# The order in which the first loads of v and of a weight stand in one DMA queue

## The chip, the cores and the metric

The kernel runs on one core of a Trainium2 chip. A core has five engines that run side by side, each with its own instruction queue and in its own order: PE (TensorE, matrix multiplies; its weight loads are listed as PEld), DVE (VectorE), ACT (ScalarE), POOL (GpSimd) and SP (SyncE), which here does nothing but issue DMA transfers. Engines wait for each other, and for transfers, by semaphores. The metric is the device time of one execution in microseconds (us); smaller is better. All times below are microseconds.

## The reference

Attention with a decay by distance for 8 batches, 8 heads, 576 positions and 64 values per head, followed by a two-layer network on the 4608 tokens that come out of it:

```python
scores = scale * np.matmul(q, k.transpose(0, 1, 3, 2))
Dmat = np.where(rel >= 0, gamma[:, None, None] ** rel[None, :, :], 0.0)
attn = np.matmul(scores * Dmat, v)            # (8, 8, 576, 64), float32
x = attn.transpose(0, 2, 1, 3).reshape(4608, 512)
h = x @ w_in                                  # w_in 512 x 2048
g = h * np.clip(h + 3.0, 0.0, 6.0) / 6.0
out = g @ w_out                               # w_out 2048 x 512
```

## The kernel before

**Tiles.** The positions of each batch are cut into four chunks of 128 and a tail of 64; two tails make one more chunk. In each chunk the scores are formed on PE (s), multiplied by a mask on DVE (into `at`), and multiplied by v and by a running state on PE (o). Its result in PSUM, `xp`, is brought by ACT into `xt` (L334), the transposed x of the batch. When the four chunks of a batch are there, the up-projection (u, or h for half of the tokens) multiplies `xt` by w_in in 16 blocks of 128 columns (fc 0 to 15); ACT and DVE make g of it (L356, L361). Then comes the down-projection: p0 to p7 for batch 0 (four accumulators in PSUM that are held until the end of p7, then copied out by ACT, L426, and DVE, L424), products P for the others.

**One written order.** There is no scheduler. The string PROGRAM is a list of short words, and `act` (L632) emits the instructions of each word in turn; each engine runs what falls to it in this order. The words that matter here:

- `L0.0` to `L1.1`: q and k of batch 0, two DMAs of 512 KB each, in runs of 1 KB (L199).
- `V0` to `V3`: v of the first four chunks, one DMA of 256 KB each, in runs of 256 bytes (`load_v`, L241), into tiles `st` of which there are six.
- `W0.i`: the i-th of eight pieces of w_in, 512 KB in runs of 2 KB (`wload`, L530). Piece i holds columns 512·(i//2) onwards (fc 4·(i//2) to 4·(i//2)+3) and half of the rows. Pieces 0 to 3 go into tiles `wst` of which there are four, pieces 4 to 7 into `tmat`, which is not yet used for anything else. `W1.i` is the same for w_out, two fc for each piece.
- `w0.ie`: the cast of such a piece to 16 bits on engine e (v DVE, s ACT, g POOL).
- `cN.2e`: the cast and scaling of chunk N's v; `cN.0e` and `cN.1e` those of its q and k. `lN`: the load of q, k and v of chunk N from 4 on (`load`, L146).
- `H19`: 19 matmuls of zeros that occupy PE while nothing has landed.

All of the loads named are issued on SP, so they stand in one queue, and the order of the words is the order of this queue. Nothing that SP issues in the first 20 us waits for another engine.

**The order around the change.** After the loads the words go on like this (left out are those that touch neither v nor w_in):

```
c0.2g c1.2g ... w0.0s K1v w0.1g ... o0 s2 o1 S3
c2.2g o2 h0.0.0.1 w0.3s c3.2g o3 h0.0.2.3 h0.1.0.1.8 w0.2g ...
w0.5g w0.6g ... h0.1.2.3 ... w0.7s ... w0.4g ... u0.4 u0.5
```

So POOL casts v0 and v1, then W0.1, then v2 and v3, then W0.2, W0.5, W0.6 and W0.4. ACT casts W0.0 before it empties `xp` of chunk 0, and W0.3 before it empties `xp` of chunk 3. The half up-projections `h0.0` need chunks 0 and 1 and the pieces 0 and 1; `h0.1` needs chunks 2 and 3 as well; `u0.4` to `u0.7` need the pieces 2 and 3, `u0.8` the pieces 4 and 5.

**Later places that are spoken of.** `c7.1v` is the cast of chunk 7's k on DVE. It is followed on DVE by `t0 t1` (differences of quarters of w_out, L576), the mask of chunk 6, and the two copies of L424; the half up-projections of batch 1 (`h1.0`) then use the PSUM buffers that these copies free. `p4` needs the cast of W1.4 on POOL.

Of the kernel before, what the change touches and what calls it, by code (L numbers as in the profile page):

```python
# [10 lines left out]
FP32 = mybir.dt.float32  # L11
# [21 lines left out]


PROGRAM = """
L0.0 L0.1 C0.0v L1.0 C0.2v L1.1 C0.1v W0.0 W0.1 V0 V1 H19 V2 V3 W0.4 W0.2
W0.3 X0.0s W0.5 C0.3g X0.1s C1.0v X0.2s X0.3s C1.1v X1.0s X1.1s C1.2v X1.2s
C1.3v X1.3s s0.4 c0.2g c1.2g W0.6 S1 K0s w0.0s K1v w0.1g W0.7 o0 s2 o1 S3
c2.2g o2 h0.0.0.1 w0.3s c3.2g o3 h0.0.2.3 h0.1.0.1.8 w0.2g W1.0 W1.6 W1.1
W1.2 W1.3 w0.5g w0.6g l4 h0.1.2.3 l5 w0.7s W1.7 W1.4 w0.4g W1.5 u0.4 u0.5  # L40
# [43 lines left out]
def kernel(  # L84
# [10 lines left out]
    B, H, S, D = q.shape  # L95
    NTOK, DM = out.shape
    DFF = moe_w_in.shape[1]
    P = 128
# [11 lines left out]
    work = ctx.enter_context(tc.tile_pool(name="work", bufs=2))  # L110
# [30 lines left out]
    stage = {}  # L141
# [1 line left out]
    v16s, s16_of, kns = {}, {}, {}  # L143
    cidx = {}

    def load(c):  # L146
        kind, b, t = c
        st = work.tile([P, 3, H, D], FP32, tag="st", bufs=6, name="st")
        stage[c] = st
        for ix, src in enumerate((q, k, v)):  # L150
            if kind == 0:
                nc.sync.dma_start(
                    st[:, ix, :, :],
                    src[b, :, t * P:(t + 1) * P, :].rearrange("h s d -> s h d"))
            else:
                for z in range(2):
                    nc.sync.dma_start(
                        st[z * TAIL:(z + 1) * TAIL, ix, :, :],
                        src[b + z, :, MAIN:S, :].rearrange("h s d -> s h d"))

    def cast(c, ix, eng):
        kind, b, t = c
        st = stage[c]
        ti = t if kind == 0 else 4
        if ix == 2:
            v16s[c] = work.tile([P, H, D], FP16, tag="v16", bufs=5, name="v16")
        elif c not in qk16s:
            qk16s[c] = work.tile([P, 2, H, D], FP16, tag="qk16", bufs=5,
                                 name="qk16")
        dst = v16s[c] if ix == 2 else qk16s[c][:, ix, :, :]  # L170
        tab = (tq if ix == 0 else tkv)[:, ti, :]
        eng.tensor_tensor(out=dst, in0=st[:, ix, :, :],  # L172
                          in1=tab.unsqueeze(2).to_broadcast([P, H, D]),
                          op=ALU.mult)

    def xpose(c):
        qk = qk16s[c]
        qt = work.tile([P, 8, P], FP16, tag="qkT", bufs=4, name="qkT")
        qkTs[c] = qt
        nc.scalar.dma_start_transpose(  # L180
            qt, qk.rearrange("p a h d -> p (a h d)"))
        kns[c] = qk[:, 1, :, :]
# [6 lines left out]
    def load0(ix, hh):  # L189
        if "st" not in qk0:  # L190
            g_new(0)
            g_new(1)
            qk0["st"] = (gs[0].rearrange("p c n -> p (c n)").bitcast(FP32)
                         .rearrange("p (a h r d) -> p a h r d", a=2, h=H, r=4))
            qk0["16"] = (gs[1][:, 0:8, :]
                         .rearrange("p (a r) n -> p a r n", a=2))
        hs = slice(4 * hh, 4 * hh + 4)
        src = (q, k)[ix][0, hs, 0:MAIN, :]
        nc.sync.dma_start(  # L199
            qk0["st"][:, ix, hs, :, :].rearrange("p h r d -> p h (r d)"),  # L200
            src.rearrange("h (p r) d -> p h (r d)", r=4))

    def cast0(ix, p0, eng):
        hs = slice(2 * p0, 2 * p0 + 2)
        tab = (tq if ix == 0 else tkv)[:, 5:9, hs].rearrange("p r h -> p h r")
        out = (qk0["16"][:, ix, :, :].rearrange("p r (h d) -> p h r d", h=H)
               [:, hs, :, :])
        eng.tensor_tensor(out=out, in0=qk0["st"][:, ix, hs, :, :],
                          in1=tab.unsqueeze(3).to_broadcast([P, 2, 4, D]),
                          op=ALU.mult)  # L210
# [7 lines left out]
    def xpose0(ix, p0, eng):  # L218
        tp = psum.tile([P, 4, P], FP16, tag="mm", bufs=4, name="tp")
        for r in range(4):  # L220
            nc.tensor.transpose(tp[:, r, :],
                                qk0["16"][:, ix, r, p0 * P:p0 * P + P], ident)
        copy(eng, wout16[:, 4 * ix + p0, :].rearrange("z (p r) -> z p r", r=4),
             tp.rearrange("z r p -> z p r"))
        if ix == 1 and p0 == 3:
            for t in range(NC4):
                qkTs[(0, 0, t)] = wout16[:, 0:8, t * P:(t + 1) * P]

    def kback(hh, eng):
        tp = psum.tile([P, 2, HP, P], FP16, tag="mm", bufs=4, name="tp")  # L230
        for a in range(2):
            t = 2 * hh + a
            for p in range(HP):
                nc.tensor.transpose(tp[:, a, p, :],
                                    wout16[:, HP + p, t * P:(t + 1) * P], ident)
            kns[(0, 0, t)] = (wout16[:, 8 + t, :]
                              .rearrange("p (h d) -> p h d", h=H))
        dst = wout16[:, 8 + 2 * hh:10 + 2 * hh, :]
        copy(eng, dst.rearrange("p a (b n) -> p a b n", b=HP), tp)

    def load_v(t):  # L241
        st = work.tile([P, 3, H, D], FP32, tag="st", bufs=6, name="st")
        stage[(0, 0, t)] = st
        nc.sync.dma_start(st[:, 2, :, :], v[0, :, t * P:(t + 1) * P, :]  # L244
                          .rearrange("h s d -> s h d"))

    def warm(ps, n, w=P):
        for _ in range(n):
            nc.tensor.matmul(ps, zero16[:, 0:P], zero16[:, 0:w], start=True, stop=True)

    def xpose_pe(c, tag, eng):
        qk = qk16s[c]
        qt = work.tile([P, 8, P], FP16, tag="qkT", bufs=4, name="qkT")
        qkTs[c] = qt
        kns[c] = qk[:, 1, :, :]
        tp = psum.tile([P, 8, P], FP16, tag=tag,
                       bufs=4 if tag == "mm" else 1, name="tp")
        qf = qk.rearrange("p a h d -> p (a h d)")
        for i in range(8):
            nc.tensor.transpose(tp[:, i, :], qf[:, i * P:(i + 1) * P], ident)  # L260
        if eng == "v":
            nc.vector.tensor_copy(qt, tp)
        else:
            nc.scalar.copy(qt, tp)
# [143 lines left out]
    def down_plain_begin(kb):  # L408
        return [psum.tile([P, DM], FP32, tag="mm", bufs=4, name="po")
                for _ in range(BLK // P)]  # L410
# [140 lines left out]
    def wcast(which, i, eng):  # L551
        st = wst.pop((which, i))
        if which == 0:
            f, cc = i // 2, i % 2
            dst = win16[:, 2 * cc:2 * cc + 2, 512 * f:512 * f + 512]
        else:
            dst = wout16[:, 2 * i:2 * i + 2, :]
        if eng == "v":
            nc.vector.tensor_copy(dst, st)
        elif eng == "s":  # L560
            nc.scalar.copy(dst, st)
        else:
            nc.gpsimd.tensor_copy(dst, st)
# [16 lines left out]
    order = []  # L580
# [51 lines left out]
    def act(w):  # L632
        kind, n, e = w[0], [int(x) for x in w[1:].rstrip("svg").split(".")], w[-1]
        if kind == "H":
            xp = psum.tile([P, HP, P], FP32, tag="xp", name="xp")
            warm(xp.rearrange("p a n -> p (a n)"), n[0], BLK)
        elif kind == "L":
            load0(*n)
        elif kind == "C":
            cast0(*n, ENG[e])  # L640
        elif kind == "X":
            xpose0(*n, e)
        elif kind == "K":
            kback(*n, e)
        elif kind == "V":
            load_v(*n)
        elif kind == "l":
            load(order[n[0]])
        elif kind == "c":
            cast(order[n[0]], n[1], ENG[e])  # L650
        elif kind == "x":
            xpose(order[n[0]])
        elif kind == "y":
            xpose_pe(order[n[0]], "xp", e)
        elif kind in "sS":
            ret1(order[n[0]], *n[1:], two=(kind == "S"))
        elif kind == "o":
            ret2(order[n[0]])
        elif kind == "W":
            wload(*n)  # L660
        elif kind == "w":
            wcast(*n, e)
        elif kind == "t":
            tbuild(n[0])
        elif kind == "e":
            enc(*n)
        elif kind == "u":
            up(*n)
        elif kind == "h":
            up_half(n[0], n[1], n[2:4], *n[4:])  # L670
        elif kind == "p":
            if n[0] == 0:
                plain.extend(down_plain_begin(0))
            down_plain_part(0, plain, 2 * n[0], 2 * n[0] + 2)
            if n[0] == HF - 1:
                down_plain_end(0, plain)
        else:
            product(n[0], PROD[n[1]])
# [31 lines left out]
```

## Time and profile before

| what | us |
|---|---|
| median of 7 runs | 308.58 |
| lowest and highest | 307.82 and 309.42 |
| the profiled execution, its own time | 309.42 |
| span of its profile | 307.3 |
| DVE, ACT, POOL busy | 240.5, 145.6, 105.2 |
| bytes moved, mean rate | 53.93 MB, 176 GB/s |

The span goes from the first to the last instruction of the profile; 2.1 us of the execution lie outside it. A busy time is the sum over an engine's instructions. On PE it is not the time at its peak, since matmuls overlap. In the lines of slices, the span is cut in 40 equal parts of 7.7 us, and each digit is a busy share in tenths (9 is 90% or more); PEclk is the share of its clock that PE was granted. In the chain of work, each line has a start, a length, and an engine with a line of the code ("SPq L244" is SP's instruction that issues a load of v); "DMA x<-y" is the time from an issue to the landing. In the waits, a line says who waited for whom, the total, how many times, and the longest. In a timeline, a line has start, length, engine, line, operation, output and input, shape and count, and in brackets the idle time before it and what ended it. In a table by windows the columns are the stretch, its length, the busy time (and instructions) of PE, PEld, DVE, ACT and POOL, PE's granted clock, the busy share of the DMA engines, and GB/s.

### The profile page before, as it was taken

How to read it: one execution, taken by the hardware profiler on the slowest of the kernel's cores; microseconds unless marked ns; L12 is line 12 of the kernel's file. 1: busy time of each engine (PE TensorE's matmuls, PEld its weight loads, DVE VectorE, ACT ScalarE, POOL GpSimd, SP SyncE). 2: the span in 40 equal slices, each digit the busy share in tenths (PEclk: the TensorE clock that was granted, in tenths of full speed). 3: DMA queues.
4: the chain of work that ended last, by engine and by line, in shares of the span. 5: the costliest groups of instructions: out<-in, count | busy, mean ns of one | idle time of the engine just before them, and what ended most of it. 6: DMA issues, size and time to landing. Idle time of an engine off the chain costs nothing.

```text
span 307.3 us, 7129 instructions
## 1 busy us (share of the span) xinstructions
PE 291.9 (95%) x2879; PEld 200.6 (65%) x2879; DVE 240.5 (78%) x341; ACT 145.6 (47%) x267; POOL 105.2 (34%) x116
## 2 busy tenths in 40 slices
PE   8788999897999799999999999999999999999995
PEld 3565444686888688746864686468755874684484
DVE  6655844989985898788878997898699768866963
ACT  2576714764135753377237522763276326405710
POOL 5055536767056745536654141333300000000000
PEclk9779999999999999999999999999999999999999
DMA  7999999999999999999999998995602030014003
GB/s 236 278 272 383 270 280 212 228 205 212 201 174 217 216 208 236 191 207 211 237 211 243 249 230 197 246 221 71 188 2 55 18 127 9 1 36 102 2 0 137
DMA packets 149728, 53.93 MB, mean 176 GB/s; under 512 B 134848, under 2 KB 145088, under 8 KB 149696
## 3 DMA queue, kind: packets, MB, share of 16 engines
q1 hardware_dynamic: 120128, 46.15, 68.7%
q10 hardware_dynamic: 29568, 7.34, 17.8%
q8 instruction: 22, 0.36, 0.5%
q14 instruction: 10, 0.08, 0.1%
HBM read 36.70 MB, written 9.44 MB: 150 GB/s over the span
## 4 chain that ended last, share of the span: by engine, by line
PE 84%; SPq 5%; DVE 4%; DMA 3%; ACT 1%; POOL 1%; issue 0%; ACTq 0%; POOLq 0%
PE ph L373 31%; PE accB L487 9%; PE accA L487 9%; PE accC L487 9%; PE ph L389 7%; PE accD L487 5%; PE po L416 4%; PE xp L304 4%; SPq L244 3%; PE sc L279 3%; DMA wst<-in_moe_w_in_dram 3%; DVE g L361 2%; PE xp L310 1%; POOL qk L172 1%; DVE ss L451 1%; PE state L329 1%
## 5 line engine op out<-in xcount | busy, mean ns | idle before, releaser
L356 ACT ACTIVATE u<-ph 128x512 f32<-128x512 f32 x144 | 84.7, 597 | 66.9 <-PE ph L373 37.1
L361 DVE SCALAR_TENSOR_TENSOR g<-u,ph 128x512 f16<-128x512 f32 x144 | 94.8, 683 | 27.4 <-ACT u L356 26.3
L373 PE MATMUL ph<-xt,win 128*128 128x512 f16 x368 | 82.1, 379 | 0.0
L373 PEld LDWEIGHTS <-win 128*128 128x128 f16 x432 | 41.4, 98 | 47.8
L487 PEld LDWEIGHTS <-ss 128*128 128x128 f16 x512 | 49.1, 98 | 6.8 <-DVE ss L451 0.8
L172 POOL TENSOR_TENSOR v<-st,tkv 128x512 f16<-128x512 f32 x29 | 33.6, 1163 | 39.8 <-DMA st<-in_v_dram 15.8
L172 POOL TENSOR_TENSOR qk<-st,tq 128x512 f16<-128x512 f32 x29 | 31.1, 1071 | 46.8 <-PE state L329 18.3
L290 DVE TENSOR_TENSOR at<-sc,mask 128x1024 f16<-128x1024 f32 (+1 forms) x34 | 39.0, 1155 | 5.7 <-PE sc L279 5.6
L487 PEld LDWEIGHTS <-g 128*128 128x128 f16 x384 | 36.9, 98 | 6.9 <-issue 1.7
L389 PE MATMUL ph<-xt,win 128*128 128x256 f16 x288 | 33.5, 274 | 2.7 <-ACT xt L334 2.7
L172 POOL TENSOR_TENSOR qk<-st,tkv 128x512 f16<-128x512 f32 x26 | 29.6, 1139 | 10.5 <-DMA st<-in_k_dram 10.3
L487 PE MATMUL accA<-wout,g 128*128 128x256 f16 x256 | 30.6, 273 | 1.7 <-DVE g L361 1.7
L389 PEld LDWEIGHTS <-win 128*128 128x128 f16 x288 | 27.7, 98 | 6.8 <-issue 3.0
L487 PE MATMUL accB<-tmat,ss 128*128 128x256 f16 x256 | 30.7, 273 | 0.1
L334 ACT ACTIVATE xt<-xp 128x512 f16<-128x512 f32 x32 | 19.1, 597 | 20.0 <-PE xp L310 17.2
L451 DVE TENSOR_TENSOR ss<-g 128x1024 f16<-128x1024 f16 (+1 forms) x30 | 23.5, 794 | 0.3
L304 PE MATMUL xp<-at,v 128*64 128x128 f16 x288 | 20.6, 228 | 1.5 <-ACT xt L334 0.8
L304 PEld LDWEIGHTS <-v 128*64 128x64 f16 x288 | 14.5, 111 | 7.3 <-issue 4.3
L507 ACT COPY osb<-accA 128x512 f32<-128x512 f32 x8 | 4.7, 586 | 28.2 <-PE accA L487 28.2
L340 ACT CAST s<-state 64x256 f16<-64x256 f32 x48 | 17.3, 361 | 0.5
L416 PE MATMUL po<-wout,g 128*128 128x512 f16 x64 | 15.0, 379 | 0.6 <-DVE g L361 0.5
L487 PE MATMUL accD<-tmat,g 128*128 128x256 f16 x128 | 15.3, 273 | 0.0
(88 smaller groups left out, 274.3 us busy)
## 6 DMA issues: line engine op xcount, KB each, us to landing
st<-in_v_dram SPq DMA_DIRECT2D x32, 256.0 KB, 6.2
out_dram<-osb SPq DMA_DIRECT2D x32, 256.0 KB, 4.5
st<-in_q_dram SPq DMA_DIRECT2D x28, 256.0 KB, 5.5
st<-in_k_dram SPq DMA_DIRECT2D x28, 256.0 KB, 5.9
wst<-in_moe_w_in_dram SPq DMA_DIRECT2D x4, 512.0 KB, 8.9
tmat<-in_moe_w_in_dram SPq DMA_DIRECT2D x4, 512.0 KB, 10.0
wst<-in_moe_w_out_dram SPq DMA_DIRECT2D x4, 512.0 KB, 10.4
g<-in_moe_w_out_dram SPq DMA_DIRECT2D x4, 512.0 KB, 6.6
```

The lines of the kernel that those rows point to most:

```text
L172: eng.tensor_tensor(out=dst, in0=st[:, ix, :, :], in1=tab.unsqueeze(2).to_broadcast([P, H, D]), op=ALU.mult)
L290: nc.vector.tensor_tensor(out=dst, in0=src, op=ALU.mult, in1=m[:, :].unsqueeze(1).to_broadcast([P, n, P]))
L304: nc.tensor.matmul(xp[rows[z], p, :], vt[:, 2 * p + z, :], at[:, z, p, :], start=(p == 0), stop=False, skip_group_check=True)
L334: nc.scalar.activation(xts[b][:, :, t * P:(t + 1) * P], xp, ACTF.Copy, scale=0.125)
L340: nc.scalar.copy(s16[rows[z], :, rows[z]], sp[rows[z], :, :])
L356: nc.scalar.activation(u, ph, ACTF.Relu, bias=0.5, scale=1.0 / 6.0)
L361: nc.vector.scalar_tensor_tensor(out=dst, in0=uv, scalar=1.0, in1=pv, op0=ALU.min, op1=ALU.mult)
L373: nc.tensor.matmul(ph, win16[:, m, P * fc:P * fc + P], xt[:, m, :], start=(m == 0), stop=(m == NCC - 1))
L389: nc.tensor.matmul(ph[:, 256 * j:256 * j + 256], win16[:, m, P * fc:P * fc + P], xt[:, m, cs], start=(m == 0 and j == 0), stop=(m == NCC - 1),
L416: nc.tensor.matmul(po, g[:, fc, P * mc:P * mc + P], wout16[:, fc, :], start=(fc == 0), stop=(fc == NFC - 1))
L451: nc.vector.tensor_tensor(out=dst, in0=a, in1=c, op=op)
L487: nc.tensor.matmul(ps[:, m, :], lhs(fc, m), rhs[:, fc, :], start=(first and fc == 0 and m == 0), stop=(fc == HF - 1 and m == 1), skip_grou ...
```

## The change

Nine words near the start of PROGRAM are put in another order: the loads of v of the first four chunks alternate with the pieces 0 to 3 of w_in, and piece 4 comes after piece 3. Beside this, `load` gets a parameter to load only one of q, k and v; no word of PROGRAM gives it.

```diff
 PROGRAM = """
-L0.0 L0.1 C0.0v L1.0 C0.2v L1.1 C0.1v W0.0 W0.1 V0 V1 H19 V2 V3 W0.4 W0.2
-W0.3 X0.0s W0.5 C0.3g X0.1s C1.0v X0.2s X0.3s C1.1v X1.0s X1.1s C1.2v X1.2s
+L0.0 L0.1 C0.0v L1.0 C0.2v L1.1 C0.1v V0 W0.0 V1 W0.1 H19 V2 W0.2 V3 W0.3
+W0.4 X0.0s W0.5 C0.3g X0.1s C1.0v X0.2s X0.3s C1.1v X1.0s X1.1s C1.2v X1.2s
...
-    def load(c):
+    def load(c, only=None):
         kind, b, t = c
-        st = work.tile([P, 3, H, D], FP32, tag="st", bufs=6, name="st")
-        stage[c] = st
+        if not only:
+            stage[c] = work.tile([P, 3, H, D], FP32, tag="st", bufs=6,
+                                 name="st")
+        st = stage[c]
         for ix, src in enumerate((q, k, v)):
+            if only is not None and ix != only:
+                continue
...
         elif kind == "l":
-            load(order[n[0]])
+            load(order[n[0]], *n[1:])
```

## The prediction

> **What bounds the kernel now.** I read the page first, then the chain of work over the first 30 us, the waits of the first 32 us, the landing of each early DMA, and last the timelines from 26 to 62 us, to see whether a gain made early survives.
>
> ```profile
> span 307.3 us, 7129 instructions
> PE 291.9 (95%) x2879; PEld 200.6 (65%) x2879; DVE 240.5 (78%) x341; ACT 145.6 (47%) x267; POOL 105.2 (34%) x116
> ...
> PEclk9779999999999999999999999999999999999999
> DMA  7999999999999999999999998995602030014003
> ```
>
> PE is the bound nearly everywhere, but the 16 DMA engines are full for the first two thirds as well. So time can be won only where PE stands still, and a win can be lost again where data come too late. PE's one long stretch of bad use is the start (slices of 7.7 us). The chain there, in order of time (start, length, what):
>
> ```profile
> 5.06 4.14 SPq L244
> ...
> 9.24 3.84 SPq L244
> ...
> 15.85 8.77 DMA wst<-in_moe_w_in_dram
> ...
> 24.64 1.04 ACT win L561
> 25.69 0.51 ACT xt L334
> ...
> 26.23 1.91 PE ph L389 x16
> ```
>
> SP is held by two loads of v (L244), then the piece W0.3 of w_in is issued at 15.85 and lands 8.77 us later; ACT casts it (w0.3s) and only then empties xp of chunk 3 (xt, L334), which stands behind the cast on ACT; PE waits for that xt. The waits (total, times, longest) price it:
>
> ```profile
> POOL v L172 <- DMA st<-in_v_dram: 7.0, 1, 7.0
> ...
> PE ph L389 <- ACT xt L334: 1.5, 1, 1.5
> ...
> ACT win L561 <- DMA wst<-in_moe_w_in_dram: 1.4, 1, 1.4
> ...
> PE xp L304 <- POOL v L172: 0.2, 1, 0.2
> ```
>
> POOL's 7.0 us for the first v costs PE 0.2; ACT's 1.4 us for W0.3 costs PE nearly all of 1.5. After 26 us PE has few waits, but DVE has a packed stretch that begins at a landing (k of chunk 7):
>
> ```profile
> 53.40 0.69 DVE L172 TENSOR_TENSOR qk<-st,tkv 128x512 f16<-128x512 f32 x1 [1.84 <-DMA st<-in_k_dram]
> 54.01 1.29 DVE L576 TENSOR_TENSOR tmat<-wout 128x1024 f16<-128x1024 f16 x2
> 55.22 2.13 DVE L576 TENSOR_TENSOR tmat<-wout,tmat 128x1024 f16<-128x1024 f16 x2
> 57.27 1.21 DVE L290 TENSOR_TENSOR at<-sc,mask 128x1024 f16<-128x1024 f32 x1
> 58.41 1.27 DVE L424 COPY osb<-po 128x512 f32<-128x512 f32 x2
> ```
>
> No gap from 53.40 to 59.68. The two copies at the end free PSUM buffers that the next up-projection needs.
>
> **What the Trainium skill says.** "DMA: Bandwidth & Descriptors", section "Queues, rings and completion order": the SP queue is one ring on each of the 16 engines, and descriptors are consumed in ring order. The trace agrees: the loads of the first 50 us, asked one by one, land in issue order. So position in the queue, not the instant of issue, decides. The same page, "Why small descriptors are slow (HBM only)", gives a 256-byte descriptor 27% of overhead; here a 256 KB load of v in 256-byte runs takes about 1.0 us of the stream (landings 14.5, 15.6, 16.4, 17.5), 512 KB of w_in in 2 KB runs about 1.35: 1.5 times as long per byte. "Perfetto Trace Analysis", DMA instruction (HWDGE), says the window of a DMA instruction is descriptor generation and not data movement; hence I go by landings.
>
> **The change part by part.** The parameter added to load() is never given, so l, c and the rest are as before; PE, ACT, DVE and POOL have the same order, and 9 SP issues change places: V0 W0.0 V1 W0.1 V2 W0.2 V3 W0.3 W0.4 for W0.0 W0.1 V0 V1 V2 V3 W0.4 W0.2 W0.3. Nothing is added or removed, and no tile gets another wait: the st and ws buffers are fresh.
>
> Landings before (issue plus its time to landing): last k 10.6, W0.0 12.0, W0.1 13.4, V0 14.5, V1 15.6, V2 16.4, V3 17.5, W0.4 20.6, W0.2 23.3, W0.3 24.6, W0.5 26.0. With 1.0 per v and 1.35 per piece from 10.6 on, the new order is V0 11.6, W0.0 13.0, V1 14.0, W0.1 15.3, V2 16.3, W0.2 17.7, V3 18.7, W0.3 20.0, W0.4 21.4, W0.5 22.7. That is a smooth stream. The old one wasn't: W0.4 and W0.2 took 5.8 us for 2.7, an excess of 3.1. If the same excess falls before W0.3, it lands at 23.1.
>
> - W0.3 earlier: ACT is free for its cast at 23.24 (u of the first up-projection, 22.64 + 0.60), against 24.64. Landing at 20.0 or at 23.1 makes no difference: ACT's whole wait goes, 1.40, and xt and PE start at about 24.85 for 26.23. Next late thing: ACT itself, so nothing over 1.4 can come from here.
> - V0 and V1 earlier: PE starts o0 at 15.70 after 0.2 of waiting, but the state matmuls after it need ACT's copy that ends at 16.02, as before. Worth 0.
> - W0.0, W0.1 later: w0.0s starts on ACT at 15.92 behind a copy; landing 13.0 is early enough. w0.1g on POOL ran 16.61 to 17.65; landing 15.3 lets it start after the casts of v0 and v1 (end 15.1). Worth 0 with no excess. Queued behind it are the casts of v2 and v3: with the whole excess of 3.1 ahead of W0.1 they end at 20.4 and about 22.8, o2 starts at 20.4 for 19.57, so at worst 0.9 of the 1.4 is lost.
> - V3 later (17.5 to 18.7): its cast ended at 19.65, now 19.8; o3 needs it at 22.53. Worth 0.
> - W0.4 later by 0.8: its cast is the last of POOL's four, end 29.35; PE wants it at u8, 31.4 before and 30.0 now. Still covered by 0.65.
>
> So PE gains 1.4 at 26 us. Does it keep it? The bytes ahead of chunk 7's k are unchanged, so with an equally good stream it still lands near 53.3 and DVE's two copies still run from 58.41. PE's second half-up of that stage starts at 59.4 (8 matmuls of 0.11 after 58.50) and needs the first copy, done at 59.1. Slack 0.4: with an unchanged stream only 0.4 of the 1.4 survives. On the way there p4 needs the cast of W1.4 (ends 47.03, p4 begins 48.45: slack 1.4, just enough). For all 1.4, the stream must be 1.0 sooner. After 62 us I find no further clip: POOL's 7.9 us wait at 84.9 is for PE's state, so loads follow PE there.
>
> How good will the stream be? The rate of the 16 engines (last figure, GB/s) while W0.4 and W0.2 followed the four v, and in the run of pieces after it:
>
> ```profile
> 17.50:20.50 3.00, 2.76 (x41) 1.91 (x42) 1.31 (x3) 1.79 (x5) 2.15 (x3) 0.66 0.92 229
> ...
> 20.50:34.00 13.50, 11.99 (x113) 7.81 (x110) 7.68 (x14) 9.39 (x17) 5.15 (x5) 0.95 1.05 374
> ```
>
> 229 for 3.0 us is 0.69 MB, which at 374 takes 1.84: a dip worth 1.16. W0.4 was issued at 14.27, soon before its turn, since SP had stood in the loads of v; in the new order W0.3 and W0.4 stand several transfers deep when their turn comes, as W0.5 and later pieces did, which ran at 1.35. I take the dip as gone or mostly so, +1.0, which keeps about 0.4 + 1.0 of the gain, at most 1.4; allowing for a partial dip I take 1.2. Bounds of the unknown: the whole 3.1 gone (no more than 1.4 counts), or a loss at each change from v to w_in (the slower rival).
>
> Sum: 309.42 in the profiled execution (span 307.3) less 1.2 is 308.2; the median of the seven runs is 0.84 lower, 308.58, so 307.4.
>
> **Rivals.**
> - Swallowed: the stream is as before and DVE's chain from k7 clips the gain to 0.4: 308.2. For it: the stream is full and its bytes are the same. Against: a visible dip exists to be won.
> - Slower: each change from 256-byte rows to a w_in piece costs. The first w_out piece after the loads of chunk 5 took 2.6 (41.9 to 44.5) for 1.35, an excess of 1.25; four such changes give 5.0 against 3.1 before, so k7 lands 1.9 later. W0.3 lands at 20.0 + 5.0 = 25.0, so the front itself is 0.4 later, and DVE frees the first buffer at 61.0 where it was 59.1 and PE could come at 59.4: 1.6 later in all, 310.2. It decides from the point where the stream is 0.4 later; at 1.0 later the price is 0.6, 309.2. Against: W0.0 after the last k, also such a change but deep in the queue, took 1.4.
> - Nothing reaches PE: the excess falls ahead of W0.1, o2 and o3 come late, the front gain is 0.5 and is then clipped to 0.4: 308.2.
> - That it doesn't do what it says is excluded: the issue order is as described.
>
> **How the numbers follow.** Forecast 0.50, swallowed 0.18, nothing 0.07, slower 0.25. A measurement here tells 0.2% (0.6 us) from no change. Faster: nearly all of the forecast and a little of the swallowed case, 0.53; same: most of swallowed and nothing and the mild end of the slower case, 0.23; slower 0.24. The forecast's own range is 306.8 to 307.9 (gain 0.7 to 1.4, and 0.4 for a stage that profits beyond my count); for 8 in 10, with part of the slower case, 306.6 to 309.8.
>
> **What would show it.** Right: ACT's wait for W0.3 gone from the waits, the xt of chunk 3 on ACT near 24.3 and PE's half-ups near 24.9; W0.3's landing before 23.2; DVE's cast of k7 starting before 53.4, by 1.0 for the full gain. Wrong: k7's cast at 53.4 with PE waiting near 59 for a buffer (swallowed); the cast later than 53.8 (slower); POOL waiting for W0.1 after 16.6 (nothing). A granted clock other than half in 18 to 22 us would shift the start by some tenths without any of these.

## The result and the profile after

| kernel | runs | median us | ratio to before, 95% interval |
|---|---|---|---|
| before | 64 | 308.09 | 1 |
| after | 27 | 306.11 | 0.993 (0.9911 to 0.9949) |
| after, measured again beside other kernels | 10 | 305.89 | 0.9908 (0.9873 to 0.9942) |

By the first ratio the change wins 2.2 us (interval 1.6 to 2.7), by the second 2.8 (1.8 to 3.9); 307.4 was forecast for 308.58, a gain of 1.2. The medians are over all runs; a ratio uses only those within 1.5% of the fastest run of their kernel. The first profile of after was taken in a run of 309.46 with three half-clock stretches and the loss near 102 that is told of below, so the profile below is that of the second measurement (its own time 305.44). The lines of the page that answer to those of before (lines of code stand 4 further down: L543 is now L547, L561 is L565, L334 is L338):

```profile
span 303.3 us, 7130 instructions
...
PE 290.3 (96%) x2879; PEld 199.4 (66%) x2879; DVE 240.0 (79%) x341; ACT 146.0 (48%) x267; POOL 103.7 (34%) x116
...
PEclk9799999999999999999999999999999999999999
DMA  7999999999999899999999999995603130013004
```

PE is busy 1.6 us less, though it does the same 2879 matmuls: it had one stretch at half clock at the start, where it had two before. The span is 4.0 us shorter, more than the medians differ. Where that goes is told below; first the same views as before. ACT around the cast of W0.3 (L565):

```profile
21.86 0.60 ACT L360 ACTIVATE u<-ph 128x512 f32<-128x512 f32 x1
22.36 1.04 ACT L565 CAST win<-wst 128x1024 f16<-128x1024 f32 x1
23.29 0.60 ACT L338 ACTIVATE xt<-xp 128x512 f16<-128x512 f32 x1
```

There is no wait ahead of the cast any more (1.40 before): W0.3 landed at 21.35 instead of 24.62. The xt of chunk 3 comes at 23.29 instead of 25.59, and PE starts its half-ups at 23.94 instead of 26.23, 2.3 earlier. The waits of the first 32 us:

```profile
POOL v L176 <- DMA st<-in_v_dram: 7.0, 3, 4.4
...
PE xp L308 <- ACT xt L338: 1.0, 2, 0.8
...
ACT win L565 <- DMA tmat<-in_moe_w_in_dram: 0.9, 1, 0.9
...
PE ph L377 <- DVE g L365: 0.4, 1, 0.4
```

PE's 1.5 for an xt is gone, but two new lines stand there: ACT waits 0.9 for a piece of w_in in `tmat`, and PE 0.4 for a g. The chain shows that they are one thing:

```profile
17.53 9.79 DMA tmat<-in_moe_w_in_dram
...
27.35 0.02 ACT win L565
...
28.30 0.60 ACT u L360
...
28.92 0.70 DVE g L365
...
29.66 2.54 PE ph L377 x11
```

W0.7 lands at 27.32, ACT casts it (w0.7s) and only then makes the u of u0.4, DVE makes its g, and this frees the PSUM buffer that u0.8 needs: PE starts u0.8 at 29.66, 2.34 after the landing. Before, it started at 31.43, and 28.63 + 2.34 = 30.97 was no limit. So of 2.3 won at 26 us, 1.8 are left here. The stream of the 16 DMA engines (last figure, GB/s):

```profile
17.50:20.50 3.00, 2.46 (x56) 1.81 (x55) 1.96 (x3) 1.71 (x5) 1.43 (x3) 1.00 0.96 287
20.50:34.00 13.50, 13.14 (x112) 7.88 (x106) 8.13 (x14) 10.94 (x19) 4.86 (x5) 1.00 1.06 359
```

The dip is smaller (287 for 229). Over all profiles of this study, the rate in 17.5 to 20.5 us was 225 to 290 with the queue of before and 287 to 378 with that of after. The stall behind the loads of v is smaller too, but not gone: W0.2 and W0.3 took 2.0 and 2.2 us each in this profile, where most later pieces took 1.3 to 1.4. The last three of the moved pieces (W0.4, W0.2 and W0.3 in the old order, W0.2, W0.3 and W0.4 in the new) took 1.5 to 3.9 us more than three times 1.35 in the eight profiles with the old queue, 3.1 in that of before, and 0.6 to 1.8 in the ten with the new one. Why a piece stalls there was not tested.

**From 26 us to the end.** PE's matmuls are the same in all kernels, so each can be set against its twin in the profile of before. In the profile of after, the distance is 2.29 at 26.23, 1.77 at 31.43, 2.08 at 76.57, 3.46 at 101.75, 3.99 at 104.12, and nearly constant from there on. Nothing is lost near 59 us, where a clip was foreseen. The 0.31 at 76.57 is a wait of PE for a g of DVE, 1.7 in before and 1.4 in after. Ahead of this g DVE makes differences of w_out (tmat) and sums of g (ss); first before, then after:

```profile
72.34 2.13 DVE L576 TENSOR_TENSOR tmat<-wout 128x1024 f16<-128x1024 f16 x2
74.39 1.52 DVE L451 TENSOR_TENSOR ss<-g 128x1024 f16<-128x1024 f16 x1
```

```profile
70.57 2.67 DVE L580 TENSOR_TENSOR tmat<-wout 128x1024 f16<-128x1024 f16 x2
73.16 0.68 DVE L455 TENSOR_TENSOR ss<-g 128x1024 f16<-128x1024 f16 x1
```

The ss took 1.52 with a cast of POOL beside it and 0.68 with none. In other profiles of either queue this wait is 0.8 or 1.7, and up to 2.1, so the 0.31 isn't counted as gain of the change. Nor are the 1.9 us that come at 102 to 104, where the change touches nothing (see chunk 10's DMA below).

### The profile page after: what moved, and what is told of

It is laid out like the page before. It is cut to its first block, busy times and chain, and to the rows that moved or that the text cites. A ratio compares the mean times of both kernels' runs of the same rounds, so it can differ in the third digit from the quotient of the medians.

```text
span 307.3 us, 7130 instructions
## 1 busy us (share of the span) xinstructions
PE 294.3 (96%) x2879; PEld 201.9 (66%) x2879; DVE 239.6 (78%) x341; ACT 145.8 (47%) x267; POOL 104.9 (34%) x116
## 4 chain that ended last, share of the span: by engine, by line
PE 88%; DVE 3%; DMA 3%; ACT 3%; POOL 1%; issue 1%; SPq 0%; ACTq 0%
PE ph L377 31%; PE accB L491 9%; PE ph L393 9%; PE accA L491 9%; PE accC L491 9%; PE accD L491 5%; PE po L420 4%; PE xp L308 4%; PE sc L283 4%; DMA g<-in_k_dram 3%; PE xp L314 2%; PE state L333 1%; DVE g L365 1%; POOL qk L176 1%; DVE ss L455 1%; ACT wout L220 1%
## 5 line engine op out<-in xcount | busy, mean ns | idle before, releaser
L365 DVE SCALAR_TENSOR_TENSOR g<-u,ph 128x512 f16<-128x512 f32 x144 | 94.9, 684 | 29.9 <-ACT u L360 28.6
L377 PEld LDWEIGHTS <-win 128*128 128x128 f16 x432 | 41.5, 98 | 47.7
L176 POOL TENSOR_TENSOR qk<-st,tq 128x512 f16<-128x512 f32 x29 | 31.5, 1086 | 48.8 <-PE state L333 17.4
L393 PE MATMUL ph<-xt,win 128*128 128x256 f16 x288 | 35.1, 281 | 2.2 <-ACT xt L338 2.2
L393 PEld LDWEIGHTS <-win 128*128 128x128 f16 x288 | 28.3, 100 | 6.7 <-issue 2.6
L338 ACT ACTIVATE xt<-xp 128x512 f16<-128x512 f32 x32 | 19.1, 598 | 20.1 <-PE xp L314 15.6
L455 DVE TENSOR_TENSOR ss<-g 128x1024 f16<-128x1024 f16 (+1 forms) x30 | 22.1, 746 | 0.3
```

What stands on the lines that cost most here:

```text
L176: eng.tensor_tensor(out=dst, in0=st[:, ix, :, :], in1=tab.unsqueeze(2).to_broadcast([P, H, D]), op=ALU.mult)
L338: nc.scalar.activation(xts[b][:, :, t * P:(t + 1) * P], xp, ACTF.Copy, scale=0.125)
L365: nc.vector.scalar_tensor_tensor(out=dst, in0=uv, scalar=1.0, in1=pv, op0=ALU.min, op1=ALU.mult)
L377: nc.tensor.matmul(ph, win16[:, m, P * fc:P * fc + P], xt[:, m, :], start=(m == 0), stop=(m == NCC - 1))
L393: nc.tensor.matmul(ph[:, 256 * j:256 * j + 256], win16[:, m, P * fc:P * fc + P], xt[:, m, cs], start=(m == 0 and j == 0), stop=(m == NCC - 1),
L455: nc.vector.tensor_tensor(out=dst, in0=a, in1=c, op=op)
```

## The experiments

Each short diff is against the kernel named. All are timed beside the kernel before, whose median was 307.9 to 308.7 from one set of runs to the next.

**1. Which part of the new order does it?** First the kernel after again, then only W0.4 moved behind W0.2 and W0.3 (w04_late), then the alternation with W0.4 left ahead of W0.2 (mix_only).

```diff
 w04_late, against before
-... W0.0 W0.1 V0 V1 H19 V2 V3 W0.4 W0.2 W0.3
+... W0.0 W0.1 V0 V1 H19 V2 V3 W0.2 W0.3 W0.4
 mix_only, against after
-... V0 W0.0 V1 W0.1 H19 V2 W0.2 V3 W0.3 W0.4
+... V0 W0.0 V1 W0.1 H19 V2 W0.4 V3 W0.2 W0.3
```

> The changed kernel once more, unchanged, for a profile with fewer half-clock windows than the first one (granted clock 0.983, three or more such windows). Front theory (only ACT's wait for W0.3 is won, at most 1.4 us): ratio 0.9955 or more. Stream theory (the earlier landings up to chunk 7's k also count): 0.993 again, with PE some 1.4 us earlier at 26 us and at 62 us. Clock theory (part of the gain is one half-clock window less, on average): 0.993, with a mean granted clock higher than before's by about 0.003 over the runs.

> The order of before with W0.4 alone put behind W0.2 and W0.3; the four v stay in one block. W0.3 has one piece of 512 KB less ahead of it and should land about 1.35 us sooner (23.3). Front theory: nearly the whole of ACT's 1.4 us wait goes and the ratio is about 0.9955 if nothing clips it. If the stretch of DVE behind chunk 7's k clips it (stream unchanged, k7 at 53.3): 0.9987. Stream theory: the stream is not improved, so 0.9985 to 1.000.

> v and w_in alternate as in the change, but W0.4 stands ahead of W0.2 and W0.3, so W0.3 has the same bytes ahead of it as before. If only the place in the queue counts: W0.3 lands near 24.6, ratio 1.000. If the alternation smooths the stream (the dip at 17.5 to 20.5 us gone): W0.3 lands near 22.4, chunk 7's k near 51.6, ratio 0.993 to 0.995 like the change.

Measured: after_again 305.89 (ratio 0.9908, 0.9873 to 0.9942); w04_late 307.41 (0.9963, 0.9938 to 0.9989); mix_only 306.93 (0.994, 0.9911 to 0.997). W0.3 landed at 21.35, 21.84 and 23.23, PE started its half-ups at 23.94, 25.31 and 24.85. By the ratios of this set w04_late wins 1.1 us and mix_only 1.9 where after wins 2.8; the intervals of mix_only and after overlap widely, so how the gain divides between the two parts is not told. In mix_only W0.3's landing still sets PE's start (the table below shows how). In w04_late it lands nearly as early as in after, and still the median is 1.5 us behind: an earlier W0.3 isn't the whole. Part of this distance is PE's clock, since the profile of w04_late had two half-clock stretches and that of after one.

**2. Does a later stream clip the gain at chunk 7's k?** The kernel after with one piece of w_out loaded twice, which puts 512 KB more ahead of all that follows.

```diff
-... w0.1g W0.7 o0 s2 o1 S3
+... w0.1g W0.7 W1.7 o0 s2 o1 S3
```

> The changed kernel with one extra load of 512 KB (W1.7, loaded a second time at its own place) behind W0.7: the front is untouched, all later landings come 1.35 us later. If DVE's stretch behind chunk 7's k clips PE: that k lands near 53.0, PE waits near 59 us, and about 0.9 of the gain is lost: ratio 0.996. If nothing after 26 us hangs on the stream: 0.993 as the change.

Measured: 306.59 (0.9946, 0.9914 to 0.9979). DVE casts chunk 7's k at 52.91 and makes the two copies (L428) that should free PE's buffers at 57.96; the lines of DVE, then those of PE:

```profile
52.91 0.73 DVE L176 TENSOR_TENSOR qk<-st,tkv 128x512 f16<-128x512 f32 x1 [1.23 <-DMA st<-in_k_dram]
...
57.96 1.27 DVE L428 COPY osb<-po 128x512 f32<-128x512 f32 x2
```

```profile
56.26 0.61 PE L264 MATMUL tp<-ident,qk 128*128 128x128 f16 x8
56.70 1.91 PE L393 MATMUL ph<-xt,win 128*128 128x256 f16 x16
58.54 0.25 PE L308 MATMUL xp<-at,v 128*64 128x128 f16 x2
```

PE runs both half-ups from 56.70 to 58.6 without a wait, while the first copy ends only near 58.6. So they wait for no buffer that DVE frees: the clip at 59 us does not exist. The time alone would not say so: 306.59 is 0.7 above after_again, near the 0.9 expected of a clip, but the intervals overlap.

**3. Is the loss near 102 us part of the gain?** In the profile of before PE waits there, and in that of after it doesn't. The first lines are before's waits in 98 to 110 us; the second and third fences are SP's waits in 70 to 92 us, before and after:

```profile
ACT u L356 <- POOL qk L172: 2.6, 1, 2.6
...
PE ph L389 <- ACT xt L334: 1.2, 1, 1.2
...
PE xp L304 <- DVE at L290: 0.5, 1, 0.5
```

```profile
SPq L400 <- DMA qkT<-qk: 6.2, 1, 6.2
```

```profile
SPq L404 <- DMA qkT<-qk: 2.3, 1, 2.3
```

SP's fourth store of batch 0 waits until chunk 10's transposing DMA (word x10, issued on ACT) has landed: in the trace of before both DMAs carry the same completion semaphore, number 108, and it goes out at 83.76, just after that landing. All later loads stand behind this store. Where SP waits 6.2 or more, POOL gets its data late, ACT stands 2.6 behind a DMA that waits for POOL's cast, and PE falls 1.9 back. If x10 is issued one place earlier on ACT, SP should wait less:

```diff
-... h1.1.6.14 h1.1.7.15 x10 c12.2g
+... h1.1.6.14 x10 h1.1.7.15 c12.2g
```

> The kernel before, with chunk 10's transposing DMA (word x10) one place earlier on ACT, ahead of the last half up-projection of batch 1 instead of behind it; all else, the order on PE, DVE, POOL and SP too, is the same. In the profile of before that DMA is issued at 76.69, lands at 83.6, and SP's fourth store of batch 0, which waits for it, goes out at 83.76 with all later loads behind it; PE then waits 1.23 and 0.46 near 102 to 104. Second-place theory (part of the gain of the change comes from there): x10 goes out near 74.3, the fourth store near 80, PE's waits near 102 are gone, 306.6 to 307.8 (0.3 to 1.7 less than before, since the profiled execution was the slowest of its seven and may lose more there than most). Front theory (all of the gain is made at 26 us): 308.1 to 308.6, no change that can be told.

> The same move of x10 in the kernel after. Second-place theory: the undisturbed profile of after shows no wait of PE near 98 to 101, so little is left to win, 305.5 to 306.0, and the distance between the two kernels with x10 moved is 1.3 to 1.8, less than the 2.2 to 2.6 between them without it. Rival (both lose there as often): after_x10 gains as much as before_x10 does, 304.5 to 305.5. Front theory: 305.9 to 306.2.

Measured: before_x10 307.8 (0.9987, 0.9967 to 1.0008), after_x10 305.22 (0.9894, 0.9858 to 0.9929). SP waits 1.7 and 2.5, and PE's waits near 102 are gone in both. The semaphore moved as well: x10 now carries 106, that of the third store, and the fourth waits for no DMA. But the distance between the two kernels is 2.6, not smaller than without the move. So the loss is no part of the change's gain: it falls in some executions of either kernel. Over the profiles without the move, PE waits 1.7 to 2.2 there in four (before, the first of after, after_cast, after_c7: SP waits 6.2 to 7.1) and not in the others, with either queue (SP waits 2.3 to 4.5). The loss goes with a wider spread: of 82 runs of three kernels with the new queue and x10 in its old place 23 took over 307 us, of 32 with x10 moved none. In the profiles chunk 10's DMA landed late (7.0 to 7.8 after its issue) only where at least one of the stores had been issued ahead of it: in four of eight such profiles, and in none of the twelve where it went out first (4.6 to 6.2). What decides among the eight was not found.

**4. Is PE's clock the missing part of the size?** Eight more matmuls of zeros ahead of chunk 2's scores, in both kernels.

```diff
-... o0 s2 o1 S3
+... o0 s2.8 o1 S3
```

> The kernel before with eight more 128x128 matmuls of zeros ahead of the scores of chunk 2, where PE waits 0.8 before o1. Clock theory (before is held at 26 us by the landing of W0.3, whatever clock PE has; after is held by PE itself): PE's half-ups start at 26.0 to 26.4 and the time is 308.0 to 308.7, unchanged. Rival (a full clock at 18 to 22 us is worth the same in both kernels): 307.3 to 307.8.

> The kernel after with the same eight matmuls of zeros. Clock theory: if they keep the clock at full in 18 to 23 us, the half-ups start at 23.5 to 24.0 and the time is 305.2 to 305.7; if the clock still falls to half there, they start near 25.2 and the time is 305.9 to 306.6. In either case the start follows PE's clock and no landing. Rival (the start in after is set by data): 23.9 or later with PE waiting for ACT or a landing, and no link to the clock.

Measured: before_warm8 307.87 (0.9986, 0.9956 to 1.0015), after_warm8 305.4 (0.992, 0.9886 to 0.9954). Before is unchanged, as the clock theory has it, and its profile shows why. It had no half clock until 25.23, and PE still waited for the xt behind W0.3's landing (24.89):

```profile
26.50 3.57 PE L389 MATMUL ph<-xt,win 128*128 128x256 f16 x16 [1.87 <-ACT xt L334]
```

But after_warm8 can't be told from after, and its profile, taken at a mean clock of 0.947, tells nothing of the start, so the half of the theory that speaks of after is not tested by this pair. The times of the runs point the same way without proving it. Of the runs of after that the ratios use, 23 with a mean clock of at least 0.993 (one half-clock stretch or none, wherever it lay) took 305.4 on average and 10 with 0.986 to 0.989 took 306.8, a difference of 1.4 give or take 0.8; of before 129 took 307.9 and 71 took 308.2, 0.3 give or take 0.35. In the other kernels with the new queue the same cut gives 0.1 give or take 1.0 (after_c7 and after_cast) and 0.7 give or take 0.7 (the four runs with x10 moved).

In two profiles with the old queue, before_warm8 and before_c7, a half-clock stretch began during or just after PE's wait for that xt (25.23 and 24.82), and u0.8 came only at 34.41 and 31.27. Whether the wait brings the half clock on is not shown; if it does, the wait costs more than its length.

**5. Take ACT's and DVE's waits for landings away, with the queue of before.** If the gain is only that casts no longer stand waiting ahead of other work, moving the casts must win as much as moving the loads. Three casts are moved, one after the other, to places where their pieces are still early enough (u0.4 is the first to read W0.3, u0.12 W0.7, p6 W1.6):

```diff
 before_cast (w0.3s); after_cast is the same in after
-... h0.0.0.1 w0.3s c3.2g o3 h0.0.2.3 h0.1.0.1.8
+... h0.0.0.1 c3.2g o3 h0.0.2.3 w0.3s h0.1.0.1.8
 before_c7, after_c7 (w0.7s); both casts: before_c37
-... l5 w0.7s W1.7 W1.4 w0.4g W1.5 u0.4 u0.5 u0.6
+... l5 W1.7 W1.4 w0.4g W1.5 u0.4 u0.5 w0.7s u0.6
 before_c376_x10 (w1.6v as well, and x10)
-... w1.1g w1.6v u0.7 w1.3g u0.8 ... u0.12 c4.0g
+... w1.1g u0.7 w1.3g u0.8 ... u0.12 w1.6v c4.0g
```

> The kernel before, its queue unchanged, with ACT's cast of W0.3 (w0.3s) behind the last half up-projection of the first two chunks, so that ACT empties chunk 3's xp ahead of the cast. Nothing on PE before u0.4 reads W0.3. Front theory (the change wins because that xt no longer stands behind the landing of W0.3; where PE starts then is set by PE and its clock): W0.3 lands at 23.5 to 25 as before, ACT's wait for it is after xt, PE starts its half-ups at 23.5 to 25.2, the time is 306.0 to 306.8. Stream theory (the smoother order of landings is what wins, at 53 us and after): k of chunk 7 lands at 53.4 as before and the time is 307.7 to 308.5. Both halves: 306.9 to 307.6.

> The kernel after with the same move of w0.3s. Front theory: W0.3 has landed before ACT needs it, so the cast's place is worth nothing beyond its own 1.04 on ACT: 305.6 to 306.2, and before_cast comes within 0.6 of it. Stream theory: 305.8 to 306.3 too, but 1.5 to 2.5 under before_cast.

> The kernel after with both moves, w0.3s behind the half up-projection and chunk 10's transposing DMA one place earlier on ACT. If the gain of x10 in the kernel after (305.22 for 306.11, six runs) holds: 304.8 to 305.4. If it was the luck of six runs: 305.6 to 306.2.

Measured: before_cast 307.31 (0.9983, 0.996 to 1.0007), after_cast 306.31 (0.9932, 0.9906 to 0.9958), after_cast_x10 305.23 (0.9909, 0.9874 to 0.9943). The front alone wins at most 1.2, perhaps nothing, and before_cast stays 1.0 behind after_cast, where the front theory had 0.6. The profile of before_cast says why; PE, then ACT:

```profile
22.35 1.91 PE L389 MATMUL ph<-xt,win 128*128 128x256 f16 x16
24.10 3.62 PE L373 MATMUL ph<-xt,win 128*128 128x512 f16 x16
30.56 5.77 PE L373 MATMUL ph<-xt,win 128*128 128x512 f16 x26 [2.84 <-DVE g L361]
```

```profile
28.24 1.04 ACT L561 CAST win<-tmat 128x1024 f16<-128x1024 f32 x1 [3.35 <-DMA tmat<-in_moe_w_in_dram]
29.20 2.05 ACT L356 ACTIVATE u<-ph 128x512 f32<-128x512 f32 x4
```

PE starts 3.9 earlier than before (no half clock in this execution), fills its four buffers, and waits 2.84 at u0.8, since ACT waits 3.35 for W0.7 (landed at 28.22). Of 3.9, 0.9 are left: the second wall is W0.7's landing, 2.34 ahead of u0.8 as in after. So:

> The kernel before, its queue unchanged, with both of ACT's casts that wait for a landing in 23 to 30 us moved behind work that doesn't need them: w0.3s behind the last half up-projection of the first two chunks, w0.7s behind u0.5. Two-walls theory (the change wins at two places of ACT, the xt of chunk 3 behind W0.3's landing and the u behind W0.7's landing, and nowhere else): with neither in the way the kernel before gains what the change gains, PE starts u0.4 at 29.0 to 30.4 for 31.43, the time is 306.0 to 306.8. Rival (the queue's order is worth something beyond those two waits, at the loads of 35 us and later): 307.0 to 307.6, as with w0.3s alone.

> The kernel before with w0.7s alone moved behind u0.5. Two-walls theory: W0.3's landing still holds PE at 26.2, and at that start W0.7 is no wait any more: 307.9 to 308.5, nothing. Rival (W0.7 is the only wall that counts): 306.3 to 307.0.

> The kernel after with w0.7s moved behind u0.5. In the undisturbed profile of after ACT waits 0.86 for W0.7, and PE's start of u0.4 keeps 1.77 of the 2.29 won at 26 us. Two-walls theory: it keeps all 2.3 when PE's clock is full, 305.3 to 305.9 (0.3 to 0.7 less than after). Rival (what is won there is lost again at a later landing): 305.9 to 306.3.

> The kernel after with w0.7s moved behind u0.5 and chunk 10's transposing DMA one place earlier on ACT. Each alone: x10 305.2; if the two add, 304.5 to 305.0; if the second is clipped by what bounds PE later, 305.0 to 305.4.

(The start that is called u0.4's there, 31.43, is u0.8's.) Measured: before_c37 306.84 (0.9972, 0.9947 to 0.9997), before_c7 307.08 (0.9996, 0.9972 to 1.0021), after_c7 305.85 (0.9927, 0.99 to 0.9954), after_c7_x10 304.77 (0.9901, 0.9864 to 0.9939). W0.7's cast alone brings nothing that can be told, both casts 0.9 by the ratio, with an interval from 0.1 to 1.6; neither theory of before_c37 is decided by that. Therefore both kernels once more without the loss near 102:

> The kernel before, its queue unchanged, with w0.3s, w0.7s and x10 all moved as in the runs before. Two-walls theory (with ACT's two waits for landings out of the way the queue's order is worth nothing more): within 0.4 of after_c7_x10, 304.6 to 305.2, and few runs over 306.5, since the loss near 102 is gone. Rival (the alternating queue is worth about 1 us beyond those two waits): 305.6 to 306.4, with PE behind after_c7_x10 by as much already at the products of batch 1.

> The same kernel as after_c7_x10, on the same chip as before_c37_x10, to set the two beside each other and to see whether the 304.8 of six runs holds. If it holds: 304.5 to 305.2. If it was the luck of six runs: 305.4 to 306.0.

Measured: before_c37_x10 306.08 (0.9937, 0.9915 to 0.9959), best_again 305.24 (0.99, 0.9872 to 0.9927). Against before_x10 (307.8, 0.9987, from another set of runs) the two casts win 1.5 to 1.7; 0.8 to 1.1 are left to the new queue (its kernel here is best_again), with intervals that overlap. The two-walls theory failed; the time is the rival's. A third wall stands in the profile of before_c37_x10; DVE, then PE:

```profile
30.49 0.69 DVE L559 CAST wout<-g 128x1024 f16<-128x1024 f32 x1 [0.51 <-DMA g<-in_moe_w_out_dram]
31.10 2.47 DVE L361 SCALAR_TENSOR_TENSOR g<-u,ph 128x512 f16<-128x512 f32 x4
```

```profile
28.42 2.76 PE L373 MATMUL ph<-xt,win 128*128 128x512 f16 x12 [0.53 <-POOL win L563]
31.83 4.48 PE L373 MATMUL ph<-xt,win 128*128 128x512 f16 x20 [0.65 <-DVE g L361]
```

DVE casts W1.6 when it lands (30.47), and the g that PE waits for stands behind it: u0.11 starts 1.36 after this landing. In best_again the piece lands at 29.45 and u0.11 starts at 30.82.

> The kernel of before_c37_x10 with a third cast moved: DVE's cast of W1.6 (w1.6v) behind the g of u0.12 instead of that of u0.6; the queue is still that of before. (In the expectations of before_c37 the start given as u0.4's is u0.8's.) In before_c37_x10 PE's u0.11 starts at 31.83, 1.36 after W1.6's landing at 30.47, and in best_again at 30.82, 1.37 after the landing at 29.45; PE is 1.0 behind from there on. Three-walls theory (what is left between the two queues passes through W1.6's landing): 305.0 to 305.6, no wait of PE at u0.11, PE at the products of batch 1 as early as in best_again but for what W0.4's later cast on POOL costs, 0.2 to 0.5. Rival (the rest of the queue's worth lies at later loads, chunk 7's k among them): 305.9 to 306.3 as in before_c37_x10.

Measured: 305.56 (0.9917, 0.9887 to 0.9947), with W0.3, W0.7 and W1.6 landing at 24.07, 28.09 and 30.80, as late as ever with the old queue. PE:

```profile
23.91 1.91 PE L389 MATMUL ph<-xt,win 128*128 128x256 f16 x16
25.66 10.52 PE L373 MATMUL ph<-xt,win 128*128 128x512 f16 x48
```

All 48 matmuls of u0.4 to u0.15 run in one piece: PE waits for none of the three landings. With its old queue and the casts out of the way, the kernel wins 2.2 over before_x10 by the ratios, and their intervals don't overlap; it comes within 0.3 of best_again by the medians and 0.5 by the ratios, less than the intervals tell. This agrees with the three-walls theory. The time alone doesn't exclude the rival, since before_c37_x10 (0.9937) lies within the interval too. At the products of batch 1 PE is 1.0 behind best_again, not 0.2 to 0.5, but this profile had a half-clock stretch at 12.0 and best_again none. The new queue with all three casts moved was not run, so it is open whether the queue is worth something beyond the three walls.

**The walls in one table.** "Half clock" is where such a stretch began before 26 us; a star marks a start that is just the landing plus 1.61 (W0.3), 2.34 (W0.7) or 1.37 (W1.6).

| profile | half clock | W0.3 | half-ups | W0.7 | u0.8 | W1.6 | u0.11 |
|---|---|---|---|---|---|---|---|
| before | 11.6, 18.4 | 24.62 | 26.23* | 28.63 | 31.43 | 31.34 | 34.02 |
| before_x10 | 11.4 (6.8 long) | 23.92 | 25.54* | 28.47 | 30.81* | 31.51 | 33.39 |
| before_warm8 | 25.2 (6.8 long) | 24.89 | 26.50* | 28.94 | 34.41 | 31.63 | 37.00 |
| before_cast | none | 22.61 | 22.35 | 28.22 | 30.56* | 30.93 | 33.15 |
| before_c37_x10 | none | 23.57 | 22.29 | 27.63 | 28.42 | 30.47 | 31.83* |
| before_c376_x10 | 12.0 | 24.07 | 23.91 | 28.09 | 29.11 | 30.80 | 31.70 |
| after_again | 10.9 | 21.35 | 23.94 | 27.32 | 29.66* | 30.47 | 32.25 |
| after_c7_x10 | 12.4, 19.2 | 20.98 | 24.36 | 26.61 | 29.56 | 29.69 | 32.15 |
| after_extra | 17.4 | 21.18 | 23.50 | 26.59 | 28.92* | 30.86 | 32.23* |
| w04_late | 13.3, 20.1 | 21.84 | 25.31 | 27.77 | 30.51 | 31.19 | 33.10 |
| mix_only | 11.2 (6.8 long) | 23.23 | 24.85* | 27.74 | 30.08* | 30.42 | 32.66 |
| best_again | none | 20.83 | 22.45 | 26.21 | 27.65 | 29.45 | 30.82* |

With W0.3 out of the way the start of the half-ups goes with PE's clock. Over all profiles it is 22.3 to 22.6 without a half-clock stretch, 23.3 to 24.1 with one and 24.4 to 25.3 with two. (Left out is after_warm8, whose clock was low throughout.)

**A better version.** The kernel after with x10 and w0.7s moved (after_c7_x10 and best_again are the same kernel) ran in 304.77 and 305.24 beside 307.9 and 308.5 for before; 0.99 (0.9872 to 0.9927) in the larger set. Beside after (0.993, 0.9911 to 0.9949) the intervals overlap; it was in no run over 306.9.

## Why the prediction was right in direction and short in size

- **ACT's wait for W0.3** (step "W0.3 earlier"): right. Its wait of 1.40 is gone in every profile with the new queue; W0.3 landed at 20.5 to 21.7, inside the 20.0 to 23.1 worked out. The stream did not become as smooth as the 20.0 supposes.
- **"Nothing over 1.4 can come from here"**: this term failed. It took ACT's 23.24 (u at 22.64) as fixed, but PE was at half clock in 18.4 to 21.85 in that one execution. Before is held by W0.3 whatever the clock; after is held by PE itself. With W0.3 early, the gain at the half-ups against the profile of before was 0.9 to 1.9 with two half-clock stretches (w04_late, the first of after, after_c7_x10), 2.1 to 2.8 with one, 3.6 to 3.8 with none. So 1.4 was a fair size for the clock of that one execution, and no bound; the prediction allowed "some tenths" for the clock. The landing varies as well: 22.6 to 24.9 with the old queue, and 24.62 is late among them. The half-ups started at 25.7 on average in the four profiles with the old queue and w0.3s in its place, and at 23.9 in seven with the new one (without after_warm8), 1.8 sooner.
- **"Slack 0.4: with an unchanged stream only 0.4 of the 1.4 survives"**, through chunk 7's k and DVE's copies: this step failed, the wait is at another place. PE waited there in no profile. The true clips are W0.7 and W1.6, with slacks before of 31.43 - 30.97 = 0.46 and 34.02 - 32.71 = 1.31. They left nothing in the waits of before, since PE came later than both.
- **"For all 1.4, the stream must be 1.0 sooner"; the dip "gone or mostly so, +1.0"**: right. Chunk 7's k landed at 52.5 on average with the old queue (seven profiles) and 51.6 with the new one (eight), W0.7 at 28.1 and 26.8, W1.6 at 30.9 and 29.9. This is what opens the second and third wall, so the earlier stream pays after all, through other casts than the one named. Why the dip shrank is open: no run set the depth of the queue apart from the alternation.
- **Sum**: 1.2 taken, 1.8 in the profile of after at u0.8, which is the slack of 0.46 and the 1.3 by which W0.7 came sooner. By 77 us it is 2.1, of which 0.3 is the wait for DVE's g; the other 1.9 of the spans is the loss near 102. That the sum, 0.4 and 1.0 for the stream, looks like these two terms is luck: its 0.4 was the slack of a wait that doesn't exist. Its cap of 1.4 was the term that made it too small.
- **W0.0, W0.1, V0, V1, V3, W0.4 at nothing**: right for after, PE has no wait for a landing of these. W0.4 does count once all else is out of the way (0.53 on POOL in before_c37_x10).
- **"After 62 us I find no further clip"**: no gain of the front was clipped there, but two waits of PE were passed over: 1.7 at 76.57 for DVE's g, and the 1.9 near 102 that 16 of the 20 profiles don't have. The distance of the profiled execution to the median, 0.84, was subtracted without asking where it lay.
- **Rivals**: none came. The pieces behind v stall less than before (0.6 to 1.8 for 1.5 to 3.9), not more; and POOL waited 0.4 for W0.1, which reached PE nowhere. (The load of w_out that the slower rival goes by took 2.7, landing at 44.58 and not 44.5.)

## What to carry to other kernels

A cast that waits for a DMA holds all that stands behind it on its engine: list, for the stage at hand, each landing plus the fixed time to the PE instruction that needs the buffer behind it, those with slack too, because the next clip is the smallest slack and shows in no wait. Moving the casts came within 0.5 of moving the loads here. And before a wait is priced from one profile, look at the clock that its neighbours ran at, and whether the profiled execution lost time elsewhere that its siblings did not.

## What was not expected of the hardware

- The same instructions ran the front up to 3 us apart, by where the half-clock stretches fell. "TensorE: Matmul & The Clock Gate" in the Trainium skill, section "What's actually happening", says that the window is free-running and lasts 3413 ns; the traces agree: the front had stretches of 3.4 or 6.8 us that began anywhere between 10.9 and 25.2, and the first profile of after one more at 102.1.
- A transposing DMA of 256 KB (chunk 10's) took 5.0 us to land in one profile and 7.8 in another of the same kernel, and through a shared completion semaphore held another queue for up to 7.1.
- DVE and POOL lengthened each other: in 72 to 76 us of before, DVE's tmat and ss (128x1024) took 1.07 and 1.52 each and POOL's casts of q and k 1.49 to 1.54 where they overlapped. Where nothing overlapped, a tmat took 0.64 (two in 1.29 in w04_late), an ss 0.68 (after), and such a cast 1.04.
